# Attention followed by an MLP on one core: layer 2 as seven half-size block products instead of eight, with block sums on VectorE and layer 1 fed with normalised rows

## The chip, the cores and the metric

The kernel runs on one core of one Trainium2 chip. The metric is the device time of one execution in microseconds (us). The runs of one kernel in one call lie within 0.2 to 2% of each other here, so times are given as the median of several runs with the lowest and highest. A run more than 1.5% above the fastest of its kernel counts as slow; there were three. They are in the medians and ranges, but not in the ratios. A ratio is the mean time of one kernel's fast runs over that of the kernel before in the same rounds on the same chip, with a 95% interval; it is therefore not quite the ratio of the medians that are quoted beside it.

Engine names in the profile: PE is TensorE (matmuls), PEld its weight loads, DVE is VectorE, ACT is ScalarE, POOL is GpSimd, SP is SyncE (DMA issue); a q behind a name marks the engine's instruction queue, and "issue" is time in which an engine waited for nothing that the profile shows. In these traces an engine works off its queue in order.

## The reference

```python
# attention: q, k, v are (8, 8, 576, 64) = batch, heads, rows, head size; a window of 64 keys, causal
scores = q @ k.T / sqrt(64);  scores = where((rel >= 0) & (rel < 64), scores, -1e9)
attn   = exp(scores - max);   attn = attn / (sum(attn) + 1e-9);   x = attn @ v     # heads joined: (8, 576, 512)
# MLP on every row of x
xn  = (x - mean(x)) / sqrt(var(x) + 1e-6) * g_ln
out = x + relu(xn @ w_ch1) @ w_ch2          # w_ch1 is (512, 2048), w_ch2 is (2048, 512)
```

## The kernel before: the parts that matter

Rows are handled in nine groups of 512: groups 0 to 7 hold the first 512 rows of the eight batch entries, and group 8 holds the 64 last rows of all eight. While the MLP of group g runs, the attention of group g+1 is woven between its matmuls: the MLP is cut into 32 units, and a small table says after which unit ("slot") which attention step is issued. The queues of all engines are filled in this order.

Layer 1 turns `zT` (rows transposed, f16) into `hrT` by 64 matmuls of 512 columns and ScalarE's Relu; layer 2 is another 64 matmuls of 512 columns.

The row scale `1/std` is not applied in front of layer 1, because it commutes with the Relu; it is applied at the very end. The gain `g_ln` is multiplied into `z`:

```python
# in b_step, after the attention output xn (128 rows) is in SBUF
nc.vector.bn_aggr(out=mvg[g][:, kb, :], in_=stats)
nc.vector.scalar_tensor_tensor(out=z, in0=xn, scalar=mvg[g][:, kb, 0:1], in1=gB,      # (x - mean) * g_ln
                               op0=ALU.subtract, op1=ALU.mult)
...
def group_stats(g, eng=nc.gpsimd):       # 1/std of 512 rows: three steps on VectorE, then Newton steps on GpSimd
    ...
    eng.tensor_scalar(out=hv, in0=mv[:, :, 1], scalar1=0.5, scalar2=0.5 * EPS, op0=ALU.mult, op1=ALU.add)
    for _ in range(2):
        eng.tensor_tensor(out=ab, in0=rs, in1=rs, op=ALU.mult)
        eng.tensor_tensor(out=ab, in0=ab, in1=hv, op=ALU.mult)
        eng.tensor_scalar(out=ab, in0=ab, scalar1=-1.0, scalar2=1.5, op0=ALU.mult, op1=ALU.add)
        eng.tensor_tensor(out=rs, in0=rs, in1=ab, op=ALU.mult)
...
def add_out(kb):                         # layer 2's result * 1/std + x
    nc.vector.scalar_tensor_tensor(out=o, in0=ch[kb], scalar=rstd[g][:, kb:kb + 1], in1=x_norm[(g, kb)],
                                   op0=ALU.mult, op1=ALU.add)
...
def w1_cast(i, eng):                     # layer 1's weights, f32 -> f16, in eight pieces of 128x1024
    nc.gpsimd.tensor_copy(out=dst, in_=t)
...
def s_mask(g, j):                        # the causal window: probabilities *= 0/1 mask, 128x1024 f16
    nc.vector.tensor_tensor(out=ptv, in0=ptv, in1=mb, op=ALU.mult)
...
# the slots of groups 2 to 6 (b = g + 1, n = g + 2)
for j in range(4):
    at(1 + 6 * j, s_mm, b, j);  at(2 + 6 * j, s_mask, b, j)
    at(7 + 6 * j, b_step, b, j);  at(min(13 + 6 * j, 29), zt_step, b, j)
at(0, group_stats, g)
at(1, load_qk, n, 0); at(2, load_qk, n, 1); at(5, load_v, n, 0, 4)
at(9, cast_qk, n, 0); at(11, cast_qk, n, 1); at(17, cast_v, n, 0, 4)        # casts, all on GpSimd
```

The softmax here doesn't subtract the row's maximum and nothing guards it: scores larger than these inputs give would overflow.

## Time and profile before

| | before |
|---|---|
| median of 3 runs | 329.69 us (328.72 to 329.92) |
| span in the profile | 328.5 us |
| TensorE busy | 314.1 us |
| VectorE, ScalarE, GpSimd busy | 163.8, 155.4, 126.4 us |
| one group in the steady part (groups 2 to 5) | 32.23 us |

The first lines are from the page of the kernel before: the span, the busy time of each engine (share of the span, instructions), and the shares of the chain of work that ended last.

```profile
span 328.5 us, 6688 instructions
PE 314.1 (96%) x2711; PEld 162.6 (49%) x2711; DVE 163.8 (50%) x307; ACT 155.4 (47%) x268; POOL 126.4 (38%) x230
PE 66%; DMA 13%; issue 8%; POOL 5%; SPq 4%; DVE 1%; ACT 1%; POOLq 0%; ACTq 0%
```

TensorE is the limit: it is busy 96% of the time, and neither VectorE nor GpSimd has more than a few per cent of the chain. The next lines are the window view of the kernel before, for group 1 and group 2. The columns are the stretch, its length, then busy time (and instructions) of PE, PEld, DVE, ACT and POOL, the granted TensorE clock, the DMA share and GB/s.

```profile
61.40:99.30 37.90, 37.10 (x426) 26.25 (x425) 26.32 (x49) 22.54 (x36) 17.21 (x30) 1.00 0.91 224
99.30:131.50 32.20, 32.20 (x273) 15.72 (x272) 16.26 (x31) 15.60 (x28) 11.96 (x23) 1.00 0.76 179
```

In group 2 TensorE has no gap at all (32.20 of 32.20 us), while VectorE has half of its time free. That free half is what the change wants to spend.

The groups view of the kernel before (line, engine, operation, output and inputs, shapes, count; then busy us and mean ns of one; then the idle time before them).

```profile
L191 POOL CAST w1g<-w2s 128x1024 f16<-128x1024 f32 x4 | 4.2, 1062 | 1.5 <-DMA w2s<-in_moe_w_ch_dram 1.5
L191 POOL CAST w1g<-w1s 128x1024 f16<-128x1024 f32 x4 | 4.2, 1061 | 2.8 <-DMA w1s<-in_moe_w_ch_dram 2.6
L292 DVE TENSOR_TENSOR pt<-pt,mask 128x1024 f16<-128x1024 f16 x28 | 19.3, 690 | 20.9 <-ACT pt L285 11.9 <-ACT pt L279 9.0
L321 DVE SCALAR_TENSOR_TENSOR z<-xn,mvg,gB 128x512 f16<-128x512 f32 x36 | 32.6, 907 | 1.3
L396 DVE SCALAR_TENSOR_TENSOR osb<-ch,rstdg,xn 128x512 f32<-128x512 f32 x36 | 27.0, 749 | 57.5 <-PE ch L387 46.1 <-issue 9.7 <-PE ch L426 1.6
```

Layer 1's weights are cast in 8.4 us of GpSimd. A mask takes 690 ns.

### The profile page before, as it was taken

The page shows a single profiled execution, that of the slowest core. Times are in us where ns is not written, and L with a number is a line of the kernel's source. Part 1 is how long each engine was busy: PE and PEld are TensorE (multiplying, and loading weights), DVE is VectorE, ACT ScalarE, POOL GpSimd, SP SyncE. Part 2 cuts the span into 40 slices and gives each one's busy share as a digit, 9 for nine tenths or more (in the row PEclk, how much of TensorE's full clock was granted, in tenths as well). Part 3 has the DMA queues.
Part 4 walks back from the last instruction along what each step waited for, and adds up shares of the span by engine and source line. Part 5 has one row for each costly group of instructions (what it writes and reads, how often), then busy time and mean ns, then how long its engine had stood idle before and what let it go on. Part 6 is the DMA issues. An engine that isn't in the chain of part 4 may idle for free.

```text
span 328.5 us, 6688 instructions
## 1 busy us (share of the span) xinstructions
PE 314.1 (96%) x2711; PEld 162.6 (49%) x2711; DVE 163.8 (50%) x307; ACT 155.4 (47%) x268; POOL 126.4 (38%) x230
## 2 busy tenths in 40 slices
PE   7989979999999999999999999999999999799993
PEld 2566435587654545454444444454445444344441
DVE  1895564584762564266526652655257713441021
ACT  2586504487636731682178217722772276216500
POOL 7566555648416501750184018301500462212000
PEclk9999989999999999999999999999999999999998
DMA  8999999976992898289938993991390397310022
GB/s 191 284 384 268 340 266 290 282 260 138 242 254 81 163 261 220 73 153 259 224 79 148 266 211 80 138 194 64 90 198 35 86 217 163 83 65 32 2 64 64
DMA packets 119329, 56.77 MB, mean 173 GB/s; under 512 B 95777, under 2 KB 112161, under 8 KB 119298
## 3 DMA queue, kind: packets, MB, share of 16 engines
q1 hardware_dynamic: 116096, 45.62, 60.2%
q0 software_dynamic: 3200, 10.72, 11.0%
q8 instruction: 21, 0.34, 0.4%
q14 instruction: 10, 0.08, 0.1%
q10 hardware_dynamic: 2, 0.00, 0.0%
HBM read 38.80 MB, written 9.44 MB: 147 GB/s over the span
## 4 chain that ended last, share of the span: by engine, by line
PE 66%; DMA 13%; issue 8%; POOL 5%; SPq 4%; DVE 1%; ACT 1%; POOLq 0%; ACTq 0%
PE ch L387 31%; PE hps L375 22%; DMA w2s<-in_moe_w_ch_dram 4%; DMA qk<-in_q_dram 4%; PE hph L411 4%; PE xps L307 3%; PE sc L275 2%; SPq L141 2%; PE ztp L332 2%; DMA w1s<-in_moe_w_ch_dram 2%; DMA tk<-in_k_dram 2%; DMA tv<-in_v_dram 1%; PE ch L426 1%; SPq L79 1%; PE tp L217 1%
## 5 line engine op out<-in xcount | busy, mean ns | idle before, releaser
L387 PE MATMUL ch<-w2s,hrT 128*128 128x512 f16 x544 | 125.0, 379 | 0.0
L375 PE MATMUL hps<-zT,w1g 128*128 128x512 f16 x480 | 109.9, 379 | 0.0
L379 ACT ACTIVATE hrT<-hps 128x512 f16<-128x512 f32 x120 | 72.0, 600 | 41.1 <-PE hps L375 40.6
L387 PEld LDWEIGHTS <-hrT 128*128 128x128 f16 x544 | 50.8, 98 | 56.4
L375 PEld LDWEIGHTS <-w1g 128*128 128x128 f16 x480 | 45.4, 98 | 54.6 <-issue 3.1
L366 POOL DMA_DIRECT2D out_dram<-osb x32 | 17.7, 554 | 130.9 <-DVE osb L396 59.4
L335 ACT COPY zT<-ztp 128x512 f16<-128x512 f16 x36 | 21.0, 583 | 77.7 <-PE ztp L332 77.5
L396 DVE SCALAR_TENSOR_TENSOR osb<-ch,rstdg,xn 128x512 f32<-128x512 f32 x36 | 27.0, 749 | 57.5 <-PE ch L387 46.1
L310 DVE RECIPROCAL rcp<-xps 128x8 f32<-128x8 f32 x36 | 7.4, 205 | 59.8 <-PE xps L307 59.8
L321 DVE SCALAR_TENSOR_TENSOR z<-xn,mvg,gB 128x512 f16<-128x512 f32 x36 | 32.6, 907 | 1.3
L292 DVE TENSOR_TENSOR pt<-pt,mask 128x1024 f16<-128x1024 f16 x28 | 19.3, 690 | 20.9 <-ACT pt L285 11.9
L128 POOL CAST qk<-qk 128x1024 f16<-128x1024 f32 x24 | 25.3, 1068 | 6.3 <-DMA qk<-in_q_dram 3.3
L285 ACT ACTIVATE pt<-sc 128x512 f16<-128x512 f32 x40 | 21.7, 596 | 12.1 <-PE sc L275 11.4
L315 DVE BATCH_NORM_STATS2 stats<-xn 128x6 f32<-128x512 f32 x36 | 25.0, 695 | 1.2
L313 DVE TENSOR_TENSOR xn<-xps,rcp 128x512 f32<-128x512 f32 x36 | 24.9, 692 | 1.2
L411 PE MATMUL hph<-zT,w1g 128*128 128x256 f16 x192 | 23.5, 273 | 1.5 <-ACT hrT L416 0.7
L411 PEld LDWEIGHTS <-w1g 128*128 128x128 f16 x192 | 18.0, 98 | 4.4 <-issue 1.8
L416 ACT ACTIVATE hrT<-hph 128x512 f16<-128x512 f32 x24 | 14.4, 599 | 10.2 <-PE hph L411 10.0
L147 POOL CAST vA<-v 128x512 f16<-128x512 f32 (+1 forms) x14 | 16.2, 1162 | 4.9 <-DMA v<-in_v_dram 4.6
L279 ACT ACTIVATE pt<-sc 128x512 f16<-128x512 f32 x32 | 17.4, 601 | 1.0
L307 PEld LDWEIGHTS <-pt 128*64 128x64 f16 x576 | 12.2, 110 | 9.2 <-issue 5.1
L209 ACT COPY qkT<-tp 128x1024 f16<-128x1024 f16 x10 | 10.0, 1012 | 11.4 <-PE tp L217 11.0
(65 smaller groups left out, 241.1 us busy)
## 6 DMA issues: line engine op xcount, KB each, us to landing
qk<-in_q_dram SPq DMA_DIRECT2D x16, 512.0 KB, 6.4
v<-in_v_dram SPq DMA_DIRECT2D x32, 256.0 KB, 5.8
out_dram<-osb POOLq DMA_DIRECT2D x32, 256.0 KB, 3.3
w2s<-in_moe_w_ch_dram SPq DMA_DIRECT2D x12, 512.0 KB, 5.9
qk<-in_k_dram SPq DMA_DIRECT2D x8, 512.0 KB, 6.9
qk<-in_k_dram SPq DMA_DIRECT2D x16, 256.0 KB, 5.8
w1s<-in_moe_w_ch_dram SPq DMA_DIRECT2D x4, 512.0 KB, 7.0
tk<-in_k_dram SPq DMA_DIRECT2D x8, 256.0 KB, 4.8
```

Source lines behind the costliest of these rows:

```text
L128: nc.gpsimd.tensor_copy(out=dst[:, :].rearrange("p (a j) e d -> p a e j d", j=j), in_=t[:, :].rearrange("p (a e j d) -> p a e j d", e=2, j ...
L285: nc.scalar.activation(out=pt[:, par], in_=sc[par], func=AF.Exp, bias=0.0, scale=scale)
L307: nc.tensor.matmul(out=xps[64 * r:64 * r + 64, h, :D + 1], lhsT=pt[:, par, hp, r, :], rhs=rhs, start=True, stop=True)
L313: nc.vector.tensor_tensor(out=xn, in0=xps[:, :, 0:D], in1=rcp_b, op=ALU.mult)
L315: nc.vector.bn_stats(out=stats, in_=xn[:, :, :].rearrange("p h d -> p (h d)"))
L321: nc.vector.scalar_tensor_tensor(out=z, in0=xn[:, :, :].rearrange("p h d -> p (h d)"), scalar=mvg[g][:, kb, 0:1], in1=gB, op0=ALU.subtract ...
L335: nc.scalar.copy(out=dst, in_=ztp)
L375: nc.tensor.matmul(out=hps, lhsT=w1g[:, kc, 128 * hc:128 * (hc + 1)], rhs=zT[g][:, kc, :], start=(kc == 0), stop=(kc == NKC - 1),)
L379: nc.scalar.activation(out=hrT[:, hc, :], in_=hps, func=AF.Relu, bias=0.0, scale=1.0)
L387: nc.tensor.matmul(out=ch[kb], lhsT=hrT[:, hc, 128 * kb:128 * (kb + 1)], rhs=w2s[:, hc, :], start=(hc == 0), stop=(hc == NHC - 1),)
L396: nc.vector.scalar_tensor_tensor(out=o, in0=ch[kb], scalar=rstd[g][:, kb:kb + 1], in1=x_norm[(g, kb)][:, :, :].rearrange("p h d -> p (h d) ...
L411: nc.tensor.matmul(out=hps[:, e], lhsT=w1g[:, kc, 128 * hc:128 * (hc + 1)], rhs=zT[g][:, kc, 256 * half:256 * half + 256], start=(kc == 0) ...
```

## The change

The intent is to take one eighth of layer 2's multiplications off TensorE. Layer 2 of a group is a product of `A` (512 rows x 2048) and `B` = `w_ch2` (2048 x 512). Each is cut in two along both axes, with `A[a][d]` for row half a and hidden half d, and `B[d][c]` for hidden half d and column half c. Eight block products give the result; Winograd's form of Strassen's method needs seven, at the price of sums of blocks:

- four sums of `B`, once for the whole kernel: T1 = B01 - B00, T2 = B11 - T1, T4 = B10 - T2, T3 = B11 - B01 (in place of B01);
- four sums of `A` per group: S1 = A10 + A11, S2 = S1 - A00, S3 = A00 - A10, S4 = A01 - S2;
- products P1 = A00 B00, P2 = A01 B10, P6 = S2 T2, P5 = S1 T1, P7 = S3 T3, P3 = S4 B11, P4 = A11 T4;
- the sums of products happen in PSUM: one bank X accumulates P1, P6, P7, P4 one after another, and after each step VectorE reads what is there (P1; P1+P6; P1+P6+P7; all four). A bank Y holds P2 and a bank Z holds P5, then P5+P3.

Sums of `A` mix rows of different scale, so the row scale can no longer wait until after layer 2; layer 1 must be fed with normalised rows. Therefore `1/std` is computed per block of 128 rows on ScalarE (logarithm and exponential of a column of 128), `z` becomes `(x - mean) * 1/std` in one VectorE tensor_scalar, and the gain `g_ln` moves into layer 1's weights, which GpSimd scales while it casts them. The Newton steps on GpSimd go. The last rows' schedule is redrawn. Group 0 keeps its eight products.

The diff, cut to its core (cuts marked):

```diff
-    def w1_cast(i, eng):
+    def w1_cast(i):
...
-            nc.gpsimd.tensor_copy(out=dst, in_=t)
+        for c in range(2):
+            kc = 2 * pr + c
+            nc.gpsimd.tensor_scalar(
+                out=w1g[:, kc, (HID // 4) * q2:(HID // 4) * (q2 + 1)], in0=t[:, c],
+                scalar1=g4[:, kc:kc + 1], scalar2=None, op0=ALU.mult,
+            )
...
+    def r_step(g, kb):
+        nc.scalar.activation(out=rs, in_=mvs[(g, kb)][:, 1:2], func=AF.Ln, bias=epst, scale=1.0)
+        nc.scalar.activation(out=rs, in_=rs, func=AF.Exp, bias=0.0, scale=-0.5)
+
+    def z_step(g, kb):
-        nc.vector.scalar_tensor_tensor(
-            out=z, in0=xn..., scalar=mvg[g][:, kb, 0:1], in1=gB,
+        nc.vector.tensor_scalar(
+            out=z, in0=x_norm..., scalar1=mv[:, 0:1], scalar2=rs[:, 0:1],
             op0=ALU.subtract, op1=ALU.mult,
         )
...
-    def group_stats(g, eng=nc.gpsimd):      # whole function, with its Newton steps on GpSimd
...
+    def t_weights(i, c):                    # half (c) of one sum of weight blocks
+        nc.vector.tensor_tensor(out=o, in0=a, in1=b, op=ALU.subtract)
+    def presum(g, i, c):                    # half (c) of one sum of hrT blocks
+        nc.vector.tensor_tensor(out=S[i], in0=a, in1=b, op=op)
+    def product(n, t):                      # 8 matmuls of 256 columns for 128 rows
+        nc.tensor.matmul(out=xyz[bank][:, t], lhsT=lhsT, rhs=rhs, start=..., stop=...)
+    def post(n, ts):                        # after a product: PSUM -> output tile, + x or + what is there
+        nc.vector.tensor_tensor(out=o, in0=xyz[bank][:, ts], in1=x if base == "x" else o, op=ALU.add)
...
+            for n in (1, 2, 6, 5, 7, 3, 4):
+                for t in range(2):
+                    units.append(lambda n=n, t=t: product(n, t))
...
+        if g == 0:
+            for n, i in enumerate((1, 2, 4)):
+                for c in range(2):
+                    at(26 + 2 * n + c, t_weights, i, c)
+        else:
+            if g == 1:
+                at(0, t_weights, 3, 0);  at(0, t_weights, 3, 1)
+            for u, i, c in ... (6, 3, 0), (10, 3, 1), (12, 1, 0), (13, 2, 0), (14, 4, 0), (16, 1, 1), (17, 2, 1), (18, 4, 1):
+                at(u, presum, g, i, c)
...
-                at(7 + 6 * j, b_step, b, j)
-                at(min(13 + 6 * j, 29), zt_step, b, j)
-        if g > 0:
-            at(4 if g == 1 else 0, group_stats, g)
+                bz(7 + 6 * j, b, j)          # b_step, then r_step and z_step one and two slots later
+                at(min(13 + 6 * j, 28), zt_step, b, j)
```

## The prediction

> **What bounds the kernel now.** TensorE. The page gives PE 314.1 of 328.5 us (96%); in the chain of waits, layer 2, layer 1 and the attention matmuls follow each other without a gap from about 70 us to 280 us. Groups 2 to 5 repeat every 32.23 us (chain of waits: layer 1 begins at 99.43, 131.66, 163.90, 196.13 us). A 128x512 matmul costs 216 ns in a stream (64 of group 8's layer 1 in 13.83 us). VectorE is busy 163.8 us (50%), ScalarE 155.4 us.
>
> **What is removed.** Layer 2 of one group is 64 matmuls of 512 columns; after, 7 x 16 = 112 matmuls of 256. The trace has such matmuls in layer 1 of group 0: 32 in 3.49 us, 109 ns each, with a fresh weight load each time, so the loads stay hidden. This agrees with the Trainium skill, "TensorE: Matmul & The Clock Gate", section "Back-to-back issue gap" (N/2.4 + 2.5 ns: 109 ns). Per group 13.83 -> about 12.1 us: 1.7 us, over eight groups 13.5 us. The new schedule of the last rows should also remove the 2.2 us that group 7 waits for a DMA transpose (timeline: idle before the scores at 283.04 us).
>
> **What is added.** VectorE per group: eight block sums of 128x1024 f16 (the mask multiply of that shape takes 690 ns): 5.5 us; seven additions out of PSUM (about 690 ns, as the xn multiply) in place of four of 749 ns: +1.8 us; z becomes a tensor_scalar, which by "VectorE: DVE Perf Modes", "The perf-mode tier table", runs fp32 SBUF data at 2x: I estimate 0.43 us for 0.91 (no run shows it yet). Net about +5 us per group. ScalarE gets two one-column operations per block (estimate 0.45 us), queued between the Relus, and they wait for VectorE's statistics.
>
> **How much is critical.** Most of the saving is given back, because the additions gather in layer 2's half of a group. From slot 13 to the group's end, groups 2 to 5 need about 16.7 us of VectorE (three attention blocks at 1.9, five sums, seven PSUM additions, two masks, three z) while TensorE needs about 16.9 us. The queue is in order, and products share PSUM banks with three additions that must read them first. Following both queues by hand with the trace's durations, I get three stalls of TensorE per group: about 0.2 us in layer 1 (Relu behind the logarithm), 0.8 us before the fifth product (the third product's addition is behind an attention block and a mask), 0.65 us before the last z transpose, now three units behind its attention block instead of four. So groups 2 to 5 gain only 0 to 0.5 us each. Groups 1 and 6, with denser VectorE work, lose 0.5 to 1 us each. Group 7 gains about 2.8 us, group 8, with an empty VectorE, 1.7 us and some 0.5 us of the tail. The ramp loses 0.5 to 1 us: weight sums, and the logarithm in a ScalarE queue that is full from 13 to 22 us.
>
> **Prediction.** 324.5 us, 8 in 10 between 317 and 330. Faster by over 2%: 0.40; within 2%: 0.55; slower: 0.05.
>
> **What would show it.** Layer 2 matmuls at 108 to 116 ns each; VectorE busy near 200 us; PE busy falling by about 13 us but idle time before products waiting for VectorE; groups 2 to 5 about 31.7 to 32.2 us apart; group 7's transpose wait gone; one activation table load.
>
> **What would make it wrong.** If additions or sums finish sooner than I queue them, groups take 30.5 us and the total nears 315. If a table load comes with every logarithm, or GpSimd scales layer 1's weights much slower than it casts them (1.04 us a piece), it is slower.

## More of the kernel before

The timeline of VectorE and GpSimd around the first mask of group 3 in the kernel before (start, duration, engine, operation; in brackets, the idle time before it and what ended it). Here and in the later timelines I show the lines that matter and leave out others between them:

```profile
166.98 0.20 POOL L355 TENSOR_TENSOR rstmp<-rstdg 128x4 f32<-128x4 f32 x1
167.41 0.69 DVE L292 TENSOR_TENSOR pt<-pt,mask 128x1024 f16<-128x1024 f16 x1 [2.24 <-ACT pt L279]
167.54 0.61 POOL L357 TENSOR_SCALAR rstmp<-rstmp 128x4 f32<-128x4 f32 x1
168.24 0.20 POOL L358 TENSOR_TENSOR rstdg<-rstdg,rstmp 128x4 f32<-128x4 f32 x1
168.37 1.04 POOL L128 CAST qk<-qk 128x1024 f16<-128x1024 f32 x1
```

The mask runs from 167.41 to 168.10. The small Newton step of GpSimd that starts during it takes 0.61 us instead of the 0.19 of its like one iteration earlier, and the first of GpSimd's large casts starts only at 168.37, after the mask.

## The result and the profile after

| | before | after |
|---|---|---|
| median | 329.21 us (328.27 to 329.92, 4 runs) | 346.63 us (346.14 to 347.6, 4 runs) |
| ratio of fast runs, 95% interval | | 1.0535 (1.0496 to 1.0573) |
| span in the profile | 328.5 us | 344.8 us |
| granted TensorE clock, mean | 0.992 | 0.973 |

The kernel after computes the right result and is 5.35% slower. The same lines of its page:

```profile
span 344.8 us, 7486 instructions
PE 306.4 (89%) x3093; PEld 201.3 (58%) x3093; DVE 228.0 (66%) x366; ACT 170.5 (49%) x340; POOL 120.2 (35%) x152
PE 58%; DVE 17%; POOL 9%; DMA 6%; SPq 3%; ACT 3%; issue 2%; DVEq 0%; POOLq 0%
```

TensorE did lose 7.7 us of work (314.1 to 306.4), but its idle time went from 14.4 us to 38.4 us (span minus busy). VectorE's share of the chain rose from 1% to 17%, and GpSimd's from 5% to 9%.

To see where, I compare when layer 1 of each group starts on TensorE (us from the start of the span) and how long each group lasts:

| | start of group 1 | group 1 | group 2 | groups 3, 4, 5 each | group 6 | group 7 | group 8 to the end |
|---|---|---|---|---|---|---|---|
| before | 61.4 | 37.9 | 32.2 | 32.2 | 33.9 | 33.4 | 32.9 |
| after | 70.3 | 49.4 | 31.2 | 32.2 | 36.1 | 29.6 | 31.5 |
| difference | +8.9 | +11.5 | -1.0 | 0.0 | +2.1 | -3.8 | -1.4 |

The differences add up to the 16.3 us between the spans. Nearly all of the loss is in the ramp (the time to the start of group 1) and in group 1. The window view of the kernel after, for groups 1, 2 and 3, in the columns explained above:

```profile
70.30:119.70 49.40, 38.56 (x473) 32.14 (x472) 40.88 (x65) 25.08 (x48) 16.76 (x22) 0.90 0.78 173
119.70:150.90 31.20, 30.77 (x320) 20.34 (x320) 23.46 (x38) 17.34 (x36) 9.06 (x12) 1.00 0.79 181
150.90:183.20 32.30, 30.93 (x323) 20.41 (x322) 25.20 (x39) 17.34 (x36) 9.06 (x12) 1.00 0.85 179
```

Group 1 has TensorE idle for 10.8 us, and it is the only one of these with a granted clock below 1. In group 3 TensorE needs 30.93 us instead of 32.20, so the saving is there, but the group takes just as long as before.

The groups view of the kernel after, for the groups that answer to those shown before, and one of the new sums:

```profile
L187 POOL TENSOR_SCALAR w1g<-w1s,g 128x512 f16<-128x512 f32 x8 | 12.5, 1576 | 0.8 <-DMA w1s<-in_moe_w_ch_dram 0.8
L187 POOL TENSOR_SCALAR w1g<-w2s,g 128x512 f16<-128x512 f32 x8 | 12.3, 1557 | 0.0
L291 DVE TENSOR_TENSOR pt<-pt,mask 128x1024 f16<-128x1024 f16 x28 | 37.0, 1320 | 19.3 <-ACT pt L278 10.6 <-ACT pt L284 8.8
L330 DVE TENSOR_SCALAR z<-xn,mv,rs 128x512 f16<-128x512 f32 x36 | 21.3, 593 | 3.2 <-ACT rs L324 3.0
L383 DVE TENSOR_TENSOR sw<-hrT 128x1024 f16<-128x1024 f16 x32 | 22.7, 712 | 15.5 <-ACT hrT L397 15.5
```

Two lines stand out. GpSimd scales the weights in 24.8 us where it cast them in 8.4. And the mask, an operation that the change did not touch, now takes 1320 ns in the mean instead of 690.

**The ramp.** GpSimd's queue is in order. In the kernel before, the first cast of group 1's q and k starts at 29.50 us; after, it stands behind the scaled weights and starts at 42.11 us. TensorE waits for it, as its timeline in the kernel after shows:

```profile
43.19 1.03 PE L216 MATMUL tp<-ident,qk 128*128 128x128 f16 x8 [3.44 <-POOL qk L126]
```

**The steady groups.** The timeline of VectorE, GpSimd and TensorE at the start of group 3 in the kernel after, to be read beside the one shown for the kernel before:

```profile
154.46 5.04 DVE L291 TENSOR_TENSOR pt<-pt,mask 128x1024 f16<-128x1024 f16 x1 [2.64 <-ACT pt L278]
152.83 1.05 POOL L126 CAST qk<-qk 128x1024 f16<-128x1024 f32 x1
153.81 1.05 POOL L123 CAST qk<-qk 128x1024 f16<-128x1024 f32 x1
...
157.07 1.88 POOL L145 CAST vA<-v 128x2048 f16<-128x2048 f32 x1
...
159.56 0.22 PE L307 MATMUL xps<-vB,pt 128*64 128x65 f16 x1 [0.98 <-DVE pt L291]
```

The mask is issued at 154.46, while GpSimd is in the middle of a run of casts, and ends at 159.50; the last cast ends at 158.95. TensorE waits 0.98 us for it. The chain of waits of the kernel after says the same for this group (start, duration, what), with the mask as a link of the chain:

```profile
151.09 1.74 PE hps L393 x8
152.85 0.60 ACT hrT L397
153.44 0.99 ACT pt L278 x2
154.46 5.06 DVE pt L291
159.56 0.45 PE xps L307 x16
```

**Group 1.** The timeline of four engines at the start of group 1 in the kernel after:

```profile
69.76 6.08 DVE L371 TENSOR_TENSOR tw<-w2s,tw 128x1024 f16<-128x1024 f16 x3
70.11 3.98 POOL L126 CAST qk<-qk 128x1024 f16<-128x1024 f32 x4
77.66 0.29 ACT L323 ACTIVATE rs<-mv,epst 128x1 f32<-128x1 f32 x1 [8.36 <-DVE mv L317]
78.10 0.58 ACT L429 ACTIVATE hrT<-hph 128x512 f16<-128x512 f32 x1
78.73 1.87 PE L424 MATMUL hph<-zT,w1g 128*128 128x256 f16 x8 [7.36 <-ACT hrT L429]
```

Three sums of weight blocks that should take 0.69 us each take 6.08 us together, while GpSimd casts. Behind them in VectorE's queue stands the statistics `mv` of an attention block. ScalarE's queue has the logarithm of this `mv` in front of a Relu, so ScalarE waits 8.36 us, and TensorE waits 7.36 us for the Relu. A 0.3 us operation on 128 numbers, put between the Relus, has coupled TensorE to VectorE's queue. The matmuls after the wait are slow as well: eight of 256 columns take 1.87 us instead of 0.87. The Trainium skill, "TensorE: Matmul & The Clock Gate", section "What's actually happening", gives a half clock after an idle window of about 3.4 us; this trace agrees, with 7.36 us idle, two such slow batches, and a granted clock of 0.50 from 78.7 to 83.0 us (0.90 in the mean of this group).

The waits view of the kernel after has one line for the logarithm and one for products that waited for an addition (who waited for whom: us in total, times, longest):

```profile
ACT rs L323 <- DVE mv L317: 38.4, 21, 8.4
PE wX L464 <- DVE osb L481: 3.5, 3, 2.3
```

ScalarE has time to spare, so most of the 38.4 us cost nothing; the longest wait, 8.4 us, cost almost all of its length. The products waited for an addition only three times: twice in group 6 (0.74 and 2.28 us at 270.4 and 276.9 us) and once in group 8 (0.52 us).

### The profile page after: what moved, and what is told of

The parts are those of the page before. It is cut to its first block, busy times and chain, and to the rows that moved or that the text cites. A ratio compares the mean times of both kernels' runs of the same rounds, so it can differ in the third digit from the quotient of the medians.

```text
span 344.8 us, 7486 instructions
## 1 busy us (share of the span) xinstructions
PE 306.4 (89%) x3093; PEld 201.3 (58%) x3093; DVE 228.0 (66%) x366; ACT 170.5 (49%) x340; POOL 120.2 (35%) x152
## 4 chain that ended last, share of the span: by engine, by line
PE 58%; DVE 17%; POOL 9%; DMA 6%; SPq 3%; ACT 3%; issue 2%; DVEq 0%; POOLq 0%
PE hps L393 24%; PE wX L464 13%; POOL w1g L187 6%; PE wZ L464 5%; DVE pt L291 5%; PE hph L424 4%; PE wY L464 4%; DMA qk<-in_k_dram 3%; PE xps L307 3%; PE sc L274 2%; DVE osb L481 2%; DVE sw L383 2%; SPq L139 2%; PE ztp L341 2%; DVE stats L315 2%
## 5 line engine op out<-in xcount | busy, mean ns | idle before, releaser
L354 POOL DMA_DIRECT2D out_dram<-osb x18 | 12.6, 697 | 154.0 <-DVE osb L481 143.5
L464 PEld LDWEIGHTS <-sw 128*128 128x128 f16 x512 | 48.7, 98 | 10.0 <-issue 3.2
L291 DVE TENSOR_TENSOR pt<-pt,mask 128x1024 f16<-128x1024 f16 x28 | 37.0, 1320 | 19.3 <-ACT pt L278 10.6
L464 PEld LDWEIGHTS <-hrT 128*128 128x128 f16 x384 | 37.1, 98 | 6.4 <-issue 0.7
L383 DVE TENSOR_TENSOR sw<-hrT 128x1024 f16<-128x1024 f16 x32 | 22.7, 712 | 15.5 <-ACT hrT L397 15.5
L323 ACT ACTIVATE rs<-mv,epst 128x1 f32<-128x1 f32 x36 | 10.6, 295 | 38.4 <-DVE mv L317 38.4
L284 ACT ACTIVATE pt<-sc 128x512 f16<-128x512 f32 x40 | 21.7, 595 | 9.1 <-PE sc L274 8.2
L210 DVE COPY qkT<-tp 128x1024 f16<-128x1024 f16 x6 | 7.3, 1225 | 27.9 <-PE tp L216 27.9
L481 DVE TENSOR_TENSOR osb<-wX,xn 128x512 f32<-128x512 f32 (+1 forms) x25 | 16.6, 664 | 11.1 <-PE wX L464 11.1
L330 DVE TENSOR_SCALAR z<-xn,mv,rs 128x512 f16<-128x512 f32 x36 | 21.3, 593 | 3.2 <-ACT rs L324 3.0
```

Of the source, the lines that this page charges most:

```text
L284: nc.scalar.activation(out=pt[:, par], in_=sc[par], func=AF.Exp, bias=0.0, scale=scale)
L383: nc.vector.tensor_tensor(out=S[i], in0=a, in1=b, op=op)
L464: nc.tensor.matmul(out=xyz[bank][:, t], lhsT=lhsT, rhs=rhs, start=bool(first and t == 0 and hc == 0), stop=(t == 1 and hc == 7), skip_grou ...
L481: nc.vector.tensor_tensor(out=o, in0=xyz[bank][:, ts], in1=x if base == "x" else o, op=ALU.add)
```

## The experiments

I had these theories, each for a part of the loss:

- **Slow scaling:** GpSimd's scaled cast takes three times as long as the plain one and delays the ramp.
- **Full VectorE** (the prediction's own theory, and a rival): there are simply too many sums and additions, and products wait for them.
- **Held by the burst:** VectorE operations with two inputs in SBUF don't run while GpSimd works off a run of casts. The Newton steps on GpSimd had kept the casts behind the first mask by accident, and the change removed them.

Eleven kernels ran, in four calls; each call had its own runs of the kernel before, with medians of 329.09, 330.09, 329.65 and 328.43 us.

| run | median us (lowest to highest) | ratio to before (95% interval) |
|---|---|---|
| e1_plain_cast | 338.76 (338.17 to 338.9) | 1.0313 (1.0273 to 1.0353) |
| e2_before_scaled_w1 | 340.53 (338.51 to 342.52) | 1.0350 (1.0290 to 1.0409) |
| e3_eight_products | 346.48 (345.94 to 347.71) | 1.0557 (1.0511 to 1.0603) |
| e4_before_newton_dve | 341.39 (340.45 to 342.11) | 1.0395 (1.0349 to 1.0440) |
| e5_hold_burst | 343.16 (342.78 to 346.07) | 1.0389 (1.0318 to 1.0460) |
| e6_weight_sums_early | 344.06 (341.58 to 346.86) | 1.0372 (1.0285 to 1.0460) |
| e7_best1 | 328.30 (327.2 to 329.76) | 0.9924 (0.9859 to 0.9989) |
| e8_newton_dve_hold | 331.31 (330.63 to 331.72) | 1.0009 (0.9942 to 1.0076) |
| e9_best2 | 328.22 (326.17 to 332.71) | 0.9944 (0.9882 to 1.0005) |
| e10_best2_eight | 333.02 (331.42 to 333.34) | 1.0100 (1.0055 to 1.0146) |
| e11_best3 | 323.37 (322.3 to 325.13) | 0.9836 (0.9792 to 0.9880) |

All gave the right result except e1, which is wrong. The ranges of e6 and e9 hold one slow run each.

### e1_plain_cast: the kernel after with layer 1's weights only cast

```diff
-        for c in range(2):
-            nc.gpsimd.tensor_scalar(out=w1g[...], in0=t[:, c], scalar1=g4[:, kc:kc + 1], scalar2=None, op0=ALU.mult)
+        nc.gpsimd.tensor_copy(out=w1g[:, 2 * pr:2 * pr + 2, ...], in_=t)
```

The gain `g_ln` is missing, so the result is wrong (relative error 0.469); the work of all other engines is the same.

> The kernel after, but layer 1's weights are only cast on GpSimd (eight casts as before), not scaled by g: the result is wrong on purpose. Theory A (the ramp is lost to GpSimd, whose 16 scaled pieces take 24.9 us in place of 8.3 us): layer 1 of group 1 begins near 62 us instead of 70.3, and the whole falls by 8 to 11 us, to 336 to 339. Rival B (the ramp is lost to the logarithm and exponential in ScalarE's queue): less than 3 us is won. What the weight sums of group 0 then collide with on GpSimd is open: the 7.4 us stall at 71 us may shrink or stay.

It took 338.76 us, 7.9 us less than the kernel after, in the expected range. The start of group 1 moved from 70.3 to 63.2 us; the 1.8 us that the ramp still loses against the kernel before have another cause. Group 1 still took 48.5 us, with a wait of 5.83 us for the Relu, and groups 3 to 5 still 32.24. So the slow scaling makes most of the ramp's loss and little else; the other half of the whole loss has another cause.

### e2_before_scaled_w1: the kernel before with layer 1's weights scaled on GpSimd

```diff
-            nc.gpsimd.tensor_copy(out=dst, in_=t)
+            nc.gpsimd.tensor_scalar(out=w1g[...], in0=t[:, c], scalar1=g4[:, kc:kc + 1], scalar2=None, op0=ALU.mult)
...
+    nc.vector.memset(g1, 1.0)      # so that gB is all ones and the result stays right
```

> The kernel before with only this part of the change: GpSimd scales layer 1's weights by g in 16 pieces, and the gain row used for z is set to ones (result right). Theory A: 8 to 11 us slower than before, near 338 to 340, and each piece takes about 1.57 us. Rival B: within 3 us of before.

It took 340.53 us, 11.4 us more than the kernel before in the same rounds, a little over what was expected. The start of group 1 moved from 61.4 to 72.0 us, with the same wait of 3.44 us for the cast of `qk`, and waits of 0.9 to 1.4 us of layer 1 of group 0 for its weights; groups 1 to 6 kept their length within 0.01 us (group 7 was 1.5 us longer in this trace, for a reason that I did not follow). Together with e1 this shows the main cause of the ramp's loss from both sides: this one edit costs 10.6 us of ramp by itself in the kernel before, and gives back 7 us in the kernel after.

### e3_eight_products: the kernel after with eight full products

```diff
-        if not two:
-            for n in (1, 2, 6, 5, 7, 3, 4): ...        # the seven products
-        for kb in range(2, 4):
+        for kb in range(2 if two else 0, 4):           # the eight products of before, in every group
...                                                     # and no block sums (t_weights, presum)
```

> The kernel after with layer 2 again as eight full products in every group (no block sums, no weight sums; normalised rows, scaled weights and the new schedule of the last rows stay; result right). It shows what the seven products themselves bring. Theory: group 1 loses its 7.4 us stall (no weight sums to be held up), each group pays 1.7 us of matmuls more, so the whole is near 340 to 346, and groups 2 to 5 repeat every 32.3 to 33.5 us against 32.24 in the kernel after. If it is faster than 338, the seven products cost more than they save.

It took 346.48 us, the same as the kernel after (346.63 in other rounds) and a little over the 340 to 346 expected. This run is the test of the theory of a full VectorE: it has none of the sums and fewer additions out of PSUM, and yet the first masks of groups 2 to 5 took 4.78 us each, and TensorE waited 0.71 us for them. This is one of them, from the timeline of VectorE in this run:

```profile
148.52 4.78 DVE L291 TENSOR_TENSOR pt<-pt,mask 128x1024 f16<-128x1024 f16 x1 [2.72 <-ACT pt L278]
```

The load of VectorE is not what made the mask slow. Groups 3 to 5 now took 33.70 us against 32.24 with seven products, so the seven products do save about 1.5 us in each of them. But group 1, which has no sums of weights in front of it now, is 8.6 us shorter (40.8 against 49.4), and group 6 is 2.0 us shorter. These effects happen to cancel.

### e4_before_newton_dve: the kernel before with the Newton steps on VectorE

```diff
-            at(4 if g == 1 else 0, group_stats, g)
+            at(4 if g == 1 else 0, group_stats, g, nc.vector)
```

> The kernel before with the small Newton steps of every group moved from GpSimd to VectorE (result right). Theory C: these steps held GpSimd's burst of casts back until the first mask multiply was done, and a VectorE operation with two inputs in SBUF that meets the burst waits for its end. Then the first mask of groups 3 to 5 takes 3 to 5 us instead of 0.69, although nothing of the Strassen products is in this kernel, and each of these groups grows by 0.5 to 1.5 us. Rival D (the 5 us belong to VectorE's own heavier load in the kernel after): the masks stay at 0.69 us and the time stays within 0.5%.

It took 341.39 us, 12.3 us more than before. The edit adds nine operations on 128x4 numbers to VectorE per group and takes them off GpSimd. This is what one of them met; the timeline of VectorE and GpSimd of this run:

```profile
170.29 0.16 DVE L350 TENSOR_TENSOR rstdg<-magt,rstmp 128x4 int32<-128x4 int32 x1
170.49 6.46 DVE L355 TENSOR_TENSOR rstmp<-rstdg 128x4 f32<-128x4 f32 x1
170.81 1.05 POOL L128 CAST qk<-qk 128x1024 f16<-128x1024 f32 x1
...
175.04 1.88 POOL L147 CAST vA<-v 128x2048 f16<-128x2048 f32 x1
176.98 0.16 DVE L356 TENSOR_TENSOR rstmp<-rstmp 128x4 f32<-128x4 f32 x1
```

An operation of 0.16 us took 6.46 us. It ended at 176.95, when the last cast ended (176.92). The mask behind it was late, and TensorE waited 2.25 us for the mask in each of the groups 3 to 5, which took 34.55 us instead of 32.23. The expectation was right about the hold but not about its victim: no mask took more than 0.69 us, because the small operation in front of it was held instead, and the groups grew by 2.3 us, not 0.5 to 1.5. No sum of blocks, no seventh product and no logarithm is in this kernel; moving a few small operations from GpSimd to VectorE is enough. The group's Newton steps on GpSimd had been of use for the time they took there.

### e5_hold_burst: the kernel after with the run of casts held behind the first mask

GpSimd gets a tiny copy of the mask that must wait until VectorE has read the old one. As the queue is in order, the casts behind it wait too. The first sum moves from slot 6 to 10, out of the reach of the casts that are now later.

```diff
                 at(2 + 6 * j, s_mask, b, j)
+                if j == 0:
+                    at(2, nc.gpsimd.tensor_copy, mask, maskc)      # maskc is a copy of mask
...
-                    (6, 3, 0), (10, 3, 1), ...
+                    (10, 3, 0), (10, 3, 1), ...
```

> The kernel after, with GpSimd's burst of casts held back in groups 2 to 5 (and the tail's in group 6) until the first mask multiply is done, by one small copy on GpSimd that rewrites the mask and so must wait for the multiply; the block sum of slot 6 moves to slot 10, out of the burst. Theory C (a VectorE operation with two SBUF inputs that meets the burst waits for the burst's end): the first masks of groups 3 to 5 fall from 5.04 to 0.69 us, the 0.98 us wait of the attention product goes, groups 3 to 5 repeat every 31.0 to 31.4 us instead of 32.24, and the whole falls by 3 to 5 us to 342 to 344. Rival D (VectorE's load makes the 5 us): the mask stays long and the time within 1 us.

It took 343.16 us (1.0389 of before, against 1.0535 for the kernel after). The timeline of VectorE and GpSimd in this run, at the start of group 3:

```profile
155.25 0.69 DVE L292 TENSOR_TENSOR pt<-pt,mask 128x1024 f16<-128x1024 f16 x1 [2.64 <-ACT pt L279]
156.01 0.24 POOL L734 COPY mask<-maskc 128x64 f16<-128x64 f16 x1 [2.38 <-DVE pt L292]
156.18 1.04 POOL L127 CAST qk<-qk 128x1024 f16<-128x1024 f32 x1
```

The mask is back at 0.69 us, groups 2 to 5 take 31.20 us each, and the wait of 0.98 us is gone. The first cast now begins 0.93 us after the mask's start, where it began 1.63 us before it in the kernel after, and in the groups 2 to 5 TensorE waited for none of the casts. Group 1, where there is no such copy, keeps its wait (7.86 us). So the steady groups' loss was the order of two queues, not an amount of work.

### e6_weight_sums_early: the kernel after with the six sums of weights three slots earlier

```diff
             for n, i in enumerate((1, 2, 4)):
                 for c in range(2):
-                    at(26 + 2 * n + c, t_weights, i, c)
+                    at(25 + (2 * n + c) // 3, t_weights, i, c)
```

> The kernel after, with the six weight sums of group 0 emitted at slots 25 and 26 instead of 26 to 31, so that they run before GpSimd's burst of four casts at 70 us. Theory C: the pair that takes 5.5 us falls to about 0.7 us each, the 7.4 us wait of group 1's second Relu falls under 2 us, and the whole falls by 4 to 7 us, to 340 to 343. If the wait only moves (another operation is caught), the time changes by less than 2 us.

The wait of 7.36 us before the second batch of layer 1 fell to 0.72, and group 1 from 49.4 to 45.9 us. But 344.06 us is only some 2.6 us less than the kernel after, less than the 4 to 7 us expected, and its runs spread widely (341.58 to 345.50 without the slow one). By the ratios, 1.0372 against 1.0535, it is faster than the kernel after; by how much stays uncertain. In the trace, group 1 started 1.1 us later, with waits of 1.12 and 0.97 us in the ramp, and there was a new wait of 2.30 us of a transpose. The sums of weights in front of the casts were the cause of the long wait, but group 1 has VectorE so full (40.9 of 49.4 us in the kernel after) that part of what is taken away in one place comes back in another.

### e7_best1: all cures together

In this version, group 0 is as it was before the change (gain in `z`, row scale at the end), so its weights only need a cast. Later, in layer 2 of group 0, ScalarE multiplies the gain into the weights in place, in four operations. The burst is held as in e5, the sums of weights are early as in e6, and the last attention block of a group is one slot earlier.

```diff
+    def w1_scale(kc):
+        nc.scalar.activation(out=w1g[:, kc, :], in_=w1g[:, kc, :], func=AF.Copy, bias=0.0, scale=g4[:, kc:kc + 1])
...
+            for kc in range(NKC):
+                at(19 + kc // 2, w1_scale, kc)
-                bz(7 + 6 * j, b, j)
+                bz(min(7 + 6 * j, 24), b, j)
```

> A first try to beat both: the kernel after with (1) group 0 as in the kernel before (gain in z, reciprocal root applied at the end), weights only cast on GpSimd and multiplied by g in place on ScalarE in group 0's layer 2, (2) the burst held as in the run above, (3) the weight sums early, (4) the last attention block of a group one slot earlier. If theory C and theory A account for the loss: group 1 begins at 61 to 63 us, lasts 38 to 41, groups 2 to 5 take 30.6 to 31.2 each, the whole 316 to 324 us, 2 to 4% faster than before. Result right.

It took 328.30 us, 0.9924 of before: the same within 2%, and short of the expected 316 to 324 us. Groups 2 to 5 took 30.62 us, with no gap over 0.3 us on TensorE. The ramp was worse than expected: TensorE waited 5.25 us at 54.56 us for a `z`, because the four scalings (2.0 us each) stood ahead of the logarithm in ScalarE's queue. This was the same mistake as in the change, made again: long work put into an in-order queue in front of a short operation that TensorE needs.

### e8_newton_dve_hold: e4 with the burst held

```diff
 # e4, and:
+                if j == 0:
+                    at(2, nc.gpsimd.tensor_copy, mask, maskc)
```

> The slow variant of the kernel before (Newton steps on VectorE in every group, 341.4 us, where one 128x4 multiply took 6.46 us) with GpSimd's burst held until the first mask is done. Theory C: all small operations take 0.16 us again, groups 2 to 5 repeat every 32.2 to 32.6 us, and the time returns to within 1.5% of the kernel before (327 to 334). If VectorE's extra work were the cause, it would stay near 341.

It took 331.31 us, the same as before (1.0009), and 10 us less than e4. The small operations took 0.16 us again, and groups 2 to 5 32.23 us. The same nine operations on VectorE are free when the casts are held back and cost 12 us when they are not.

### e9_best2: e7 with the scalings spread

```diff
-                at(19 + kc // 2, w1_scale, kc)
+            at(17, w1_scale, 0);  at(23, w1_scale, 2);  at(24, w1_scale, 1);  at(30, w1_scale, 3)   # no. 2 on VectorE
...                            # the last rows' first attention block moves from group 6 to group 7;
...                            # three block sums and the last attention block of group 1 are moved too
```

> The second try to beat both. Against the first (328.3 us): the multiplications of the weights by g are spread over group 0's layer 2 (three on ScalarE, one on VectorE) instead of four in a row, which held a transpose of group 1 back by 5.25 us; group 1's block sums no longer stand ahead of its z; the first block of the last rows moves from group 6, where VectorE is full, to group 7. Expected: group 1 begins at 61.5 to 63.5 us (67.5 in the first try) and lasts 37.5 to 40 us (41.2), groups 6 and 7 together take 61.5 to 63 us (64.4), groups 2 to 5 stay at 30.6, the whole 315 to 321 us. Result right.

The median was 328.22 us, and its best run 326.17. The profiled run fell in the slow state (332.71), so its absolute gaps in groups 1 and 7 are not used here; groups 2 to 5 took 30.62 us in it. Against e7 nothing certain was gained, and the expected 315 to 321 us were missed.

### e10_best2_eight: e9 with eight products

```diff
-            for n in (1, 2, 6, 5, 7, 3, 4): ...
+        for kb in range(2 if two else 0, 4): ...
```

> The same kernel with layer 2 as eight full products in every group, without weight sums and block sums: everything else equal. It shows what the seven products bring once the collisions are gone. If they bring what the matmul count says, less small stalls: groups 2 to 5 at 31.8 to 32.3 us against 30.6, the whole 9 to 13 us slower than the seven products (326 to 332). If VectorE's extra work takes it back: less than 5 us of difference.

It took 333.02 us (1.0100 of before), against 0.9944 for e9 in the same rounds. The groups 2 to 5 took 32.32 us against 30.62. That is what the seven products save together with their sums and additions, which e10 leaves out, while the other parts of the change stay on both sides: 1.70 us per group. The prediction had 1.7 for the matmuls alone. Over the whole kernel the difference is only about 5 us (4.8 by the medians, 5.1 by the ratios), not the 9 to 13 expected, though the groups 2 to 5 alone give 6.8. In group 1 nothing is gained: it took 40.56 us in e10 and 41.18 in e11, which has seven products and four more edits. So in these runs the seven products pay in groups 2 to 5, where TensorE has no wait, but not in group 1.

### e11_best3: the ramp and the last rows tidied

Four edits on e9: group 0 shares the output tiles of the pairs, so that a store is not waited for; one evacuation of a transpose goes from VectorE to ScalarE; the last scaling is two slots earlier; and the loads of the last rows are issued earlier.

```diff
-                at(30, w1_scale, 3)
+                at(28, w1_scale, 3)
-            at(27, t_main, 1, 1, 1, 1)
+            at(27, t_main, 1, 1, 1, 0)
-            o = p_blk.tile([128, DM], FP32, tag="osb1", ..., bufs=2)
+            o = oo[kb // 2][:, kb % 2]              # half of a pair's tile
-            ... (20, load_tail, 2) ...              # group 6; load_tail 3 at slot 0 of group 7
+            ... (15, load_tail, 2) ... (26, load_tail, 3) ...
```

> The third try to beat both. Against the second (328.2 us): group 0's outputs use four half tiles of the pair buffer instead of two single ones (VectorE waited 3.57 us there for a store, and GpSimd's burst behind it slipped into group 1's statistics), one transpose of group 1 is copied out by ScalarE, the loads of the last two tails are issued ahead of the transposes they queued behind. Expected: group 1 begins at 60 to 61.5 us and lasts 38.5 to 42 us (45.7 in the profile of the second try), groups 6 and 7 take 62 to 64 us together (69.3 there), groups 2 to 5 stay at 30.6, the whole 316 to 323 us, 2 to 4% faster than before. Result right.

It took 323.37 us over 6 runs (0.9836, interval 0.9792 to 0.9880): 1.6% faster than the kernel before (whether by 2% is left open by the interval) and 6.6% faster than the kernel after, by its ratio over theirs. The expected 316 to 323 us were just missed. The busy times from its page:

```profile
PE 301.5 (94%) x3095; PEld 199.5 (62%) x3095; DVE 213.0 (66%) x382; ACT 176.0 (55%) x336; POOL 105.9 (33%) x149
```

Its window view, for groups 1 and 3:

```profile
63.20:104.40 41.20, 36.20 (x474) 30.80 (x473) 35.09 (x60) 25.29 (x48) 12.75 (x18) 1.00 0.83 189
135.00:165.60 30.60, 30.60 (x322) 20.33 (x320) 21.36 (x39) 17.35 (x36) 9.39 (x13) 1.00 0.87 189
```

Group 3 has no idle time on TensorE (30.60 of 30.60) at a VectorE that is busy 21.36 of 30.60 us. Group 1 is still 3.3 us longer than in the kernel before (41.2 against 37.9), with 5 us idle, and the ramp 1.8 us longer (63.2 against 61.4); together these give back 5.1 us of what the other groups gain (6.4 us in groups 2 to 5, and 5.4 us in groups 6 to 8).

## Why the prediction was wrong

It said 324.5 us, with 317 to 330 as the range; it was 346.63 us. Point by point:

- **The arithmetic saved was right.** 16 matmuls of 256 columns took 1.75 us in groups 2 to 8, 109 ns each; the prediction named 108 to 116. This agrees with the figure that it took from the Trainium skill; the page ("TensorE: Matmul & The Clock Gate", section "Back-to-back issue gap") gives that formula for an isolated matmul and warns that it miscounts in a stream with weight loads, but these streams agree with it (109 ns for 256 columns, 216 for 512). The saving of 1.7 us per group was measured as 1.70 (e10 against e9). TensorE's busy time fell by 7.7 us in place of 13; in group 1 it even rose, from 37.10 to 38.56 us, at a lower granted clock (0.90). In e11 it fell by 12.6 us.
- **The step that failed first: "The ramp loses 0.5 to 1 us".** It lost 8.9 us. The prediction costed the weight sums and the logarithm there, but not the scaling on GpSimd. It did name "GpSimd scales layer 1's weights much slower than it casts them" among what would make it wrong, but gave it no time in the sum and only 5% to "slower". The measured term: 16 operations of 1.57 us in place of 8 of 1.06, so 24.8 us against 8.4; e2 gives 10.6 us of ramp for it alone. Without it (e1), the ramp loses 1.8 us, still more than was costed.
- **The second: "Groups 1 and 6, with denser VectorE work, lose 0.5 to 1 us each".** Group 1 lost 11.5 us. Its mechanism was not a dense VectorE alone but weight sums that met a run of GpSimd casts (6.08 us for three), and ScalarE's in-order queue that carried the delay to a Relu and so to TensorE; e6 moved the sums and 7.36 us of wait became 0.72. Group 6 lost 2.1 us, and here the prediction's own theory did show: VectorE had no pause over 0.1 us from 260.4 to 277.9, and the fifth product waited 2.28 us for the third product's addition, which stood behind an attention block and a mask, as the prediction had it, with 0.8 us, for groups 2 to 5. In the same stretch four VectorE operations were held up by GpSimd casts, for 2.8 us together; how much of the wait is a full queue and how much these holds was not separated.
- **The third, hidden by a right number: "groups 2 to 5 gain only 0 to 0.5 us each".** They gained 1.0, 0, 0 and 0. But the reason given, three stalls through a full VectorE queue, was mostly not there. The stalls of 0.2 us in layer 1 and of 0.8 us before the fifth product did not occur in groups 2 to 5, and of the 0.65 us before the last `z` transpose 0.40 was seen. The main stall, 0.98 us, was for the mask, and its cause was the interplay of two engines that the prediction did not mention at all (e3 against "too much work on VectorE"; e4, e5 and e8 for "held by the burst"). A number that fits doesn't prove the reason behind it.
- **Groups 7 and 8.** A gain of 2.8 us was predicted for group 7; 3.8 was measured, and the wait of 2.2 us for a transpose is gone. For group 8 some 2.2 us were predicted and 1.4 measured; the last product still waits 0.52 us for an addition.
- **Sizes.** The new `z` took 0.593 us in the mean and 0.55 undisturbed, in place of the estimated 0.43; logarithm and exponential 0.50 us together; VectorE's busy time was 228.0 us in place of 200, of which 17.7 us is the longer time of the masks alone (37.0 in place of 19.3). As said there, there was one table load.
- **Where the sum was mis-sized.** Taking the middle of its ranges, the prediction is 8.2 us short in the ramp, 10.8 in group 1 and 1.4 in group 6, and it is 0.2 off in groups 7 and 8 together. These 20 us are nearly the whole 22 us between 324.5 and 346.63.

The missing rule could have been read. The Trainium skill, "SBUF — State Buffer", section "Who interferes with whom", says that VectorE and GpSimd share a pair of SBUF ports: a VectorE instruction with two SBUF inputs contends with a GpSimd instruction that reads SBUF, and so does one in a 2-port mode; whoever issues first has the ports, and the other waits. The traces agree with it. Masks and sums, with two SBUF inputs, were held (5.04 us, 1.52 us), and so was the new `z` (1.39 us), which has one SBUF input and so, by the page, would have to be in a 2-port mode; the profile does not show the mode. Operations that read PSUM (`xn`, 692 and 691 ns in the mean before and after, and `osb`, 664) and the statistics, with one SBUF input (695 ns in both), were not. And where VectorE came first, GpSimd waited: the Newton step of 0.61 us in the kernel before. The sign of it stood in the profile of the kernel before, as `z` at 907 ns against `osb` at 749. That the ports are what holds an operation is the page's account: the runs show who is held and when, not the ports.

What stays open: why the scaled cast on GpSimd is so slow. When exactly a held operation is let in between two GpSimd operations was not tested either: the long holds shown above lasted to the last cast of a run, but other operations were let in after the first cast. In the kernel after, the weight sum at 60.38 us and the block sum of 1.52 us at 260.98 us ended 0.54 us after the first cast of a run, and the second cast took 1.49 us in place of 1.04 in the latter case; e5 has the same at 60.50 and 262.00 us. In e11, why group 1 still has some 5 us of gaps was read from the trace (waits for `z`, for sums and for evacuations, none over 1.8 us) but not tried.

## What to carry to other kernels

Before moving work to an engine with spare time, look at which other engine shares its memory ports and at what that engine does at that moment: on this chip a VectorE operation with two SBUF inputs can wait for a whole run of GpSimd work (6.46 us in e4), so place it before such a run or hold the run back behind it. Before changing the operation that an engine performs on its way (a scaled cast in place of a cast), find or measure its duration, and follow the in-order queue behind it; a risk that is named but not costed is not in the prediction. Removing instructions can also take away a delay that some other part depended on, so ask what each removed instruction had been holding back.

## What the Trainium skill lacked or had wrong

- "SBUF — State Buffer", section "Who interferes with whom": it says that the one which comes second waits until the first instruction has finished. In these runs, the VectorE operation was often not let in between the instructions of a run on GpSimd: the mask of 0.69 us took 5.04 us, from the second cast of five to the end of the last, in the kernel after, though only a memset of 0.32 us lay between the second and the third; a 128x4 operation of 0.16 us took 6.46 us across five casts in e4, although by the profile's start times it began 0.32 us ahead of the first (GpSimd was issuing a DMA then, from 170.27 to 170.81 us). The held 128x1024 and 128x512 operations ended 0.54 to 0.55 us after the end of the last cast of the run (masks at 159.50, 162.86 and 146.11 us in the kernel after, e5 and e11; `z` at 260.10 us in the kernel before). Some operations were let in after the first cast (above), and the page does not say which of the two is to be expected.
- "GPSIMD Engine Reference", section "4.1 Engine selection": it calls elementwise work with one input roughly line-rate on GpSimd. A cast of 128x512 f32 to f16 took 617 ns here, but a tensor_scalar of the same shape and types with a scalar for each partition took 1557 to 1576 ns. The page has no figure for it.
- "VectorE: DVE Perf Modes", section "The perf-mode tier table": the prediction's estimate from the 2x rate for a tensor_scalar of fp32 data in SBUF, 0.43 us for 128x512, was too low; undisturbed it took 0.55 us, against 0.75 for the old `z`. Whether it ran at 2x is not shown by the runs.
- "VectorE: DVE Perf Modes", section "The DRAIN you can't avoid": it says that the next operation doesn't start until the pipe is empty, and adds that one which isn't held starts earlier, without a figure. In the kernel after, sums and additions that follow each other without dependence start every 0.60 us although each of them lasts 0.68 to 0.69; the prediction had added up the full durations, which may be one reason why the stall before the fifth product did not come in groups 2 to 5 (not tested).
